# First transform of batch 0 with x as the stationary operand, its result kept on chip

## The chip, the cores and the metric

One core of a Trainium2 chip runs the whole program. The metric is the time on the device of one execution, in microseconds (us), lower is better. TensorE is called PE (its weight loads PEld), VectorE DVE, ScalarE ACT, GpSimd POOL and SyncE SP; SBUF is the memory on the chip, PSUM the accumulators that TensorE writes, DRAM the memory off the core.

## The reference

A two-dimensional Fourier transform of x, of which the real part is kept, is followed by two layers of two matrix products each.

```python
batch, seq, dim = (2, 3008, 256)
X = np.fft.fft(x, axis=1)
X = np.fft.fft(X, axis=2)
x = X.real.reshape(6016, 256)
h = x @ w_in                                     # 256 -> 2048
x = (np.maximum(h, 0.0) + alpha * np.minimum(h, 0.0)) @ w_out
h = x @ w_in2
out = (h * (1.0 / (1.0 + np.exp(-h)))) @ w_out2  # 2048 -> 256
```

## The kernel before, in words

The sequence transform of length 3008 = 47 * 64 is done as a transform of length 47 (stage A), one of length 64 (stage B), and the transform along the 256 columns is folded into the first weight matrix (`mix_w`: every pair of row blocks of `w_in` is multiplied with `cwt`). By symmetry 24 of the 47 rows and half of the columns are computed, in NC = 6 blocks c of 8 rows each: blocks 0 to 2 are batch 0, blocks 3 to 5 batch 1. A block has 512 columns of tokens, block 0 only 450.

Products of the layers are made in float32r in three passes: each operand is split in a high part (a copy by ACT into float32r) and a low part (the subtraction of the two on DVE or POOL). A float32 matmul that isn't split stands in the profile as two passes, each with a weight load of its own.

Before the loop over the blocks there is a front that prepares batch 0:

- Ten matmuls on zeros (`spin`) run while the first transfers land. Eight x tiles of 96 partitions x 1024 (`x`, 384 KB each) are loaded on SP's queue.
- Stage A, for each tile: ACT copies the high part (`xh`, L942), DVE subtracts the low part (`xl`, L943), PE makes 3 matmuls for each half tile with the constant `cat` as the stationary operand (`psA`, L355 to L357), ACT and DVE copy the result into `ev` (L960, L962).
- The result has the wrong axis on the partitions, so it goes through DRAM: `save_a` writes `tmid[0]`, `load_ur` reads it back turned as `ur` (in the place of `pq` of block 5). The table `QUEUE` says behind which tile each of these transfers is issued. The parts for blocks 1 and 2 are saved later (`save_a` with part 1 behind the loads of the front, `put` for part 2 in the loop) and loaded by `stage_b` with `load_u`.
- The first column pair of `w_in`, p = 0, is loaded as 64-bit words (`raw`), narrowed to float32 (`narrow`: ACT L211, L212, then DVE L217, L219, L221), and mixed (`psW` L512, `psS` L518). Fourteen and eight further `spin` matmuls stand around it.
- Stage B of block 0: 16 float32 matmuls `psB` (L984) with `ur` stationary, their split into `pq` (ACT L991, DVE L993), a row built on POOL (L979) and summed over the partitions by PE (`psP`, L995), copied into `pb`.

The loop `step1(c, m)` then runs 16 steps m for each block: 6 matmuls `psh` (L556), on DVE and ACT the activation (L564 to L570), `gh` and `gl` split on ACT and POOL (L586, L587), and 12 matmuls `pso` (L602) into `po`. Beside the steps of block 0 run what the later steps need, as jobs that `at(step, ...)` plans and that go on at named phases of a step: narrowing and mixing p = 2 to 7 of `w_in`, narrowing `w_out` in eight parts n (`narrow_wout`; part 0 at step 0; its split is ACT L265, POOL L266), stage B of block 1 (`stage_b` at steps 3, 6, 7, 9, then `rank_one`, which makes `pb` of block 1 through a small tensor `rd` in DRAM). Every engine works in the order in which the program is written. After the six blocks the second layer follows, in the same way.

Of the kernel before, what the change touches and what calls it, by code (L numbers as in the profile page):

```python
# [69 lines left out]
def _constants():  # L70
# [24 lines left out]
def kernel(  # L95
# [8 lines left out]
    ca: bass.AP,  # L104
    cb: bass.AP,
# [13 lines left out]
    psh = ctx.enter_context(tc.tile_pool(name="psh", bufs=1, space=PSUM, reuse_waits="tile"))  # L119
    pso = ctx.enter_context(tc.tile_pool(name="pso", bufs=4, space=PSUM, reuse_waits="tile"))  # L120

    tmid = [dram.tile([N2, 2 * CK * 2, P], F32, name=f"tmid{c}") for c in range(NC)]
# [9 lines left out]

    def place_pq(c):
        if c not in pq:
            pq[c] = keep.tile([P, 4, CK * N2], F32R, name=f"pq{c}", tag=f"px{c}")
        return pq[c]
# [196 lines left out]
    cbt = pf.tile([P, 2, N2], F32, name="cbt")  # L333
# [58 lines left out]
    def products_b(u):  # L392

        ps = ptile([P, KG, 2, N2], "psB")
        for k in range(KG):
            for eo in range(2):
                T.matmul(ps[:, k, eo], u[:, eo, k, :], cbt[:, eo], start=True, stop=True)  # L397
        return ps
# [21 lines left out]
    def stage_b(c, kk):  # L420
        while c >= NC // 2 and len(saved) < N2 // 4:
            yield EARLY
# [10 lines left out]
        pairs = list(parts_b(c, kk, products_b(u)))  # L433
# [15 lines left out]
    def rank_one(c):  # L449
# [4 lines left out]
        T.matmul(ps, u0, cbt[:, 0], start=True, stop=True)  # L454
# [44 lines left out]
    def mix_w(p, pool=None, tag="x"):  # L499
# [23 lines left out]
        if p < 2:  # L523

            column(pso.tile([P, 2, 2], F32, name="psS", tag="o"))
# [301 lines left out]
    def start_win2():  # L827
# [21 lines left out]
    SPIN = 10, 14, 8  # L849

    QUEUE = ((("s", 0, 8),), (("s", 8, 16),), (("s", 16, 24), ("w",), ("b",)), (("s", 24, 32), ("p", 0)),
             (("l", 0, 16, 0), ("s", 32, 40)), (("l", 16, 32, 0), ("s", 40, 48)), (("s", 48, 56), ("l", 32, 48, 0)),
# [288 lines left out]
```

## Time and profile before

| | |
|---|---|
| time, median of 3 runs | 984.4 us (982.74 to 984.95) |
| profiled execution: span from first to last instruction | 984.3 us |
| profiled execution: time of its own | not listed apart from the span |
| PE busy | 954.4 us, 97% of the span |
| PEld, DVE | 791.0 and 719.7 us |
| ACT, POOL | 598.0 and 508.6 us |
| moved by DMA | 52.72 MB |

The page names, for each engine, its busy time; the windows cut the span into stretches and give busy time and the granted TensorE clock of each; the chain follows the work that ended last back from the end; the timeline lists instructions in order of their start, with the idle time before them and what released them in brackets.

### The profile page before, as it was taken

To read this page: it belongs to the slowest core of one execution; us is meant where nothing else is said; L and a number is where in the kernel's file an instruction comes from. 1 tells how busy PE (TensorE), PEld (TensorE's weight loads), DVE (VectorE), ACT (ScalarE), POOL (GpSimd) and SP (SyncE) were. 2 spreads that over 40 slices of the span, in tenths; PEclk is the share of its full clock that TensorE was granted. 3 is DMA by queue.
4 is the path that set the end of the run, shared out by engine and by line. 5 is a ranking of instruction groups with operands and counts; after the bars stand their busy time and mean duration, and the time that the engine had idled before them with its cause. 6 is when DMAs were issued, how large, how long until landed. Compare 5 with 4: busy or idle time off the path is not lost.

```text
span 984.3 us, 12429 instructions
## 1 busy us (share of the span) xinstructions
PE 954.4 (97%) x4316; PEld 791.0 (80%) x4316; DVE 719.7 (73%) x1103; ACT 598.0 (61%) x1006; POOL 508.6 (52%) x328
## 2 busy tenths in 40 slices
PE   8799999999999999999999999999999999999998
PEld 5688878878878878778789988888888888888886
DVE  6698876778989989998766766576576566657554
ACT  6566566666656656665676565665566565556654
POOL 0154567765445556988996553354354354335322
PEclk9899999999999999999999999999999999999999
DMA  8921133323333220010011020010001001001001
GB/s 227 309 96 49 31 90 79 88 71 95 107 118 112 81 65 22 22 65 22 11 44 33 0 81 1 1 43 1 1 0 43 1 1 43 1 1 43 1 1 44
DMA packets 39407, 52.72 MB, mean 54 GB/s; under 512 B 3792, under 2 KB 22064, under 8 KB 39088
## 3 DMA queue, kind: packets, MB, share of 16 engines
q1 hardware_dynamic: 39056, 51.60, 17.1%
q8 instruction: 34, 0.56, 0.2%
q10 hardware_dynamic: 288, 0.33, 0.1%
q14 instruction: 29, 0.24, 0.1%
HBM read 35.26 MB, written 16.66 MB: 53 GB/s over the span
## 4 chain that ended last, share of the span: by engine, by line
PE 75%; DVE 9%; DMA 5%; ACT 4%; POOL 3%; issue 2%; SPq 1%; ACTq 0%; POOLq 0%; DVEq 0%
PE pso L790 26%; PE psh L722 23%; PE pso L602 15%; PE psh L556 8%; DVE r L570 4%; POOL gl L587 2%; ACT r L566 2%; DMA tmid<-ev 1%; DVE psh L565 1%; DMA stash_i<-y 1%; DMA stash_o<-y 1%; PE psB L397 1%; DMA raw<-in_w_in 1%; DVE h L564 1%; DVE y L221 1%
## 5 line engine op out<-in xcount | busy, mean ns | idle before, releaser
L743 DVE TENSOR_TENSOR ring<-ring,psh 128x512 f32<-128x512 f32 (+1 forms) x336 | 222.2, 674 | 167.5 <-PE psh L722 158.3
L790 PE MATMUL pso<-ghl,wAo 128*128 128x512 f32 (+1 forms) x1152 | 309.8, 385 | 0.0
L587 POOL TENSOR_TENSOR gl<-r,gh 128x1024 fp32r<-128x1024 f32 (+1 forms) x96 | 227.0, 2365 | 152.5 <-ACT gh L586 97.5
L722 PE MATMUL psh<-ts,wi 128*128 128x512 f32 (+1 forms) x1008 | 279.0, 385 | 0.0
L734 POOL TENSOR_TENSOR ghl<-ring,ghl 128x512 fp32r<-128x512 f32 (+1 forms) x96 | 137.1, 1429 | 252.6 <-ACT ghl L729 172.7
L790 PEld LDWEIGHTS pso<-ghl,wAo 128*128 128x128 f32 x1152 | 216.2, 188 | 40.7
L746 ACT ACTIVATE ring<-ring 128x512 f32<-128x512 f32 (+1 forms) x192 | 119.4, 622 | 176.4 <-DVE ring L743 174.6
L722 PEld LDWEIGHTS psh<-ts,wi 128*128 128x128 f32 x1008 | 189.1, 188 | 35.5 <-DVE r L570 0.3
L602 PE MATMUL pso<-gh,wo_o 128*128 128x512 f32 (+1 forms) x768 | 188.8, 386 | 3.0 <-POOL wo_o L266 2.9
L556 PE MATMUL psh<-pq,wa 128*128 128x512 f32 (+1 forms) x576 | 167.6, 400 | 4.7 <-DVE r L570 4.4
L602 PEld LDWEIGHTS pso<-gh,wo_o 128*128 128x128 f32 x768 | 144.2, 188 | 31.8 <-POOL wo_o L266 4.5
L570 DVE SCALAR_TENSOR_TENSOR r<-r,al,psh 128x512 f32<-128x512 f32 (+1 forms) x192 | 134.0, 734 | 17.8 <-ACT r L566 6.9
L586 ACT ACTIVATE gh<-r 128x1024 fp32r<-128x1024 f32 (+1 forms) x96 | 100.3, 1045 | 69.5 <-DVE r L570 69.1
L556 PEld LDWEIGHTS psh<-pq,wa 128*128 128x128 f32 x576 | 105.5, 190 | 29.7 <-DVE r L570 10.8
L729 ACT ACTIVATE ghl<-ring 128x512 fp32r<-128x512 f32 (+1 forms) x192 | 118.9, 619 | 6.2
L602 PE MATMUL pso<-gl,wo_o 128*128 128x512 f32 (+1 forms) x384 | 103.0, 390 | 2.9 <-POOL gl L587 2.9
L566 ACT ACTIVATE r<-psh 128x512 f32<-128x512 f32 (+1 forms) x96 | 56.5, 588 | 80.2 <-DVE psh L565 70.3
L565 DVE TENSOR_TENSOR psh<-h,psh 128x512 f32<-128x512 f32 (+1 forms) x96 | 65.8, 685 | 42.8 <-PE psh L556 37.4
L602 PEld LDWEIGHTS pso<-gl,wo_o 128*128 128x128 f32 x384 | 72.4, 189 | 18.5 <-POOL gl L587 4.6
L734 DVE TENSOR_TENSOR ghl<-ring,ghl 128x512 fp32r<-128x512 f32 (+1 forms) x96 | 77.2, 804 | 4.0 <-ACT ghl L729 3.5
L564 DVE SCALAR_TENSOR_TENSOR h<-pb,wst,psh 128x512 f32<-128x512 f32 (+1 forms) x96 | 69.9, 729 | 3.1 <-DMA pb<-rd 3.1
L567 DVE TENSOR_TENSOR psh<-h,psh 128x512 f32<-128x512 f32 (+1 forms) x96 | 65.2, 679 | 0.0
(94 smaller groups left out, 681.0 us busy)
## 6 DMA issues: line engine op xcount, KB each, us to landing
raw<-in_w_in SPq DMA_DIRECT2D x16, 512.0 KB, 6.2
raw<-in_w_out SPq DMA_DIRECT2D x16, 512.0 KB, 3.9
ur<-tmid SPq DMA_DIRECT2D x20, 256.0 KB, 3.3
out_dram<-ob SPq DMA_DIRECT2D x20, 256.0 KB, 2.2
tmid<-ev SPq DMA_DIRECT2D x50, 64.0 KB, 1.8
x<-in_x SPq DMA_DIRECT2D x8, 384.0 KB, 8.0
xr<-in_x SPq DMA_DIRECT2D x16, 192.0 KB, 2.4
tmid<-ev SPq DMA_DIRECT2D x23, 128.0 KB, 5.7
```

Of the source, the lines that this page charges most:

```text
L556: T.matmul(t[:, :w], wa[q][:, mm, eo, a, :], pq[c][:, 2 * eo + bb, :w], start=n == 0, stop=n == 2)
L564: V.scalar_tensor_tensor(t[:, :w], pb[c][:, :w], wst[:, m, 0:1], ps[0][:, :w], op0=ALU.mult, op1=ALU.add)
L570: V.scalar_tensor_tensor(r[:, s, :w], r[:, s, :w], al[:, m:m + 1], ps[s][:, :w], op0=ALU.mult, op1=ALU.add)
L586: A.activation(hi[:, :, :w], r[:, :, :w], AF.Copy)
L587: G.tensor_tensor(lo[:, :, :w], r[:, :, :w], f32(hi[:, :, :w]), op=ALU.subtract)
L602: T.matmul(po[c][s][k][:, :w], wo1[q][:, mm, a, k * P:(k + 1) * P], g[:, s, :w], start=m == 0 and a == 0 and g is hi, stop=m == NF - 1 and ...
L722: T.matmul(bank[j][:, :w], wi2[p][:, FORMS[j], a], t[:, :w], start=a == 0 and t is hi, stop=t is lo)
L729: A.activation(outs[p, i][:, 0, :w], g[:, :w], AF.Copy)
L734: eng.tensor_tensor(hl[:, 1, :w], g[:, :w], f32(hl[:, 0, :w]), op=ALU.subtract)
L743: V.tensor_tensor(dst[:, :w], a[:, :w], bank[j][:, :w], op=ALU.add)
L746: A.activation(a[:, :w], a[:, :w], AF.Silu)
L790: T.matmul(po[c, 2][s][k][:, :w], wo2[q][:, mm + m, a, k * P:(k + 1) * P], outs[p, i][:, g, :w], start=p == 0 and i < 2 and a == 0 and g == 0,
```

## The change

Stage A of batch 0 is turned round. The x tile is the stationary operand, in float32 and unsplit, and the constant (`a0`, 96 x 96) is the moving one, so that the result has the axis on the partitions that stage B wants. There are 64 such matmuls of 96 columns (`stage_u`, `psU`), in five units of 12 and one of 4; after each unit four copies (two on DVE, two on ACT, 64 partitions x 48 x n) put them into `u_all`, which holds blocks 0 to 2 on chip until step 26 of the loop (`set_apart` then gives its place to `pq` of blocks 3 to 5). The writes to and reads from `tmid` of blocks 0 to 2 go, and with them `ev`, the splits `xh` and `xl`, `QUEUE`, `put`, and the second and third group of `spin`. `tmid` stays for batch 1.

`cbt` gets a second form for the row order that results (`cbts`, 128 KB). The constants `cwt` and `cbts` are loaded on ACT's queue at the very start instead of behind the third tile. On SP's queue p = 0 of `w_in` stands behind the sixth x tile (`BEHIND`), and behind the eighth all other raw weights follow without waiting for anything. Part 0 of `w_out` is narrowed and split in the front (`wo0`), ahead of stage B's split, no longer at step 0. `take_in` moves from step 14 to step 27. `stage_b` of blocks 1 and 2 loads nothing, so it is one phase shorter.

```diff
+    a0 = a.reshape(2 * NP1, H1 // CK, 2, 2, CK).transpose(0, 2, 1, 3, 4).reshape(2 * NP1, -1).astype(np.float32)
...
+    three = tc.tile_pool(name="three", bufs=1, side="right", reuse_waits="tile")
+    u_all = three.__enter__().tile([P, 3, 2, CK, P], F32, name="u_all")
...
-        while c >= NC // 2 and len(saved) < N2 // 4:
+        while c >= HOST and len(saved) < N2 // 4:
...
-        u = pf.tile([P, 2, KG, P], F32, name="ur", tag="ur", bufs=2)
-        load_u(c, kk, u)
-        yield EARLY
+        if c < HOST:
+            u = u_all[:, c, :, kk:kk + KG]
+        else:
+            u = pf.tile([P, 2, KG, P], F32, name="ur", tag="ur", bufs=2)
+            load_u(c, kk, u)
+            yield EARLY
...
-    SPIN = 10, 14, 8
-
-    QUEUE = ((("s", 0, 8),), (("s", 8, 16),), (("s", 16, 24), ("w",), ("b",)), (("s", 24, 32), ("p", 0)),
...
+    SPIN = 10,
+
+    BEHIND = 5
+    UNITS = 12, 12, 12, 12, 12, 4
...
+        ac = wtile([2 * NP1, 2 * NP1], F32, "const", "y")
+        nc.sync.dma_start(ac, a0)
...
+            nc.sync.dma_start(xr[i], x[0, i])
+            if i == BEHIND:
+                next(first[0])
+        A.dma_start(cwt.rearrange("p k e j -> p (k e j)"), cw)
+        A.dma_start(cbts.rearrange("p a e k -> p (a e k)"), cb)
+        load_raw("o", 0)
+        next(first[1])
...
+        for kind, n in RAW_ORDER:
+            load_raw(kind, n)
...
+        def stage_u(n):
...
+            t = pp.tile([P, 3, 512], F32, name="psU", tag="u", bufs=2)
+            for j in range(n):
+                i, r = divmod(done + j, NX)
+                T.matmul(t[:, j // 4, j % 4 * 96:j % 4 * 96 + 96], xr[i][:, r], ac, start=True, stop=True)
+            v = t[:, :n // 4, :384].rearrange("p b (j m c) -> p b j m c", j=4, m=2)
+            for i, (half, m) in enumerate(((0, 0), (1, 0), (0, 1), (1, 1))):
+                src = v[half * N2:(half + 1) * N2, :, :, m].rearrange("p b j c -> p c b j")
+                dst = uv[m * N2:(m + 1) * N2, :, half, done:done + n].rearrange("p c (b j) -> p c b j", j=4)
+                if i % 2:
+                    A.activation(dst, src, AF.Copy)
                 else:
+                    V.tensor_copy(dst, src)
+            done += n
+
+        for i, n in enumerate(UNITS):
+            stage_u(n)
+            if i == 3:
+                run(first[0])
+            if i == 4:
+                run(mix_w(0, pp, "o"))
...
+        wo0 = narrow_wout(w_out, wo1, "wo1_", 0, 0, raws["o", 0])
...
+        run(wo0)
+        ur, cbt = u_all[:, 0], side(0)
...
-        for n in range(8):
+        for n in range(1, 8):
             at(WOUT[n], narrow_wout, w_out, wo1, "wo1_", n, 0, raws.get(("o", n)))
-        for i, n in enumerate(SAVES):
-            at(n, put, i)
-        at(14, take_in)
+        at(26, set_apart)
+        at(27, take_in)
```

On PE, the end of the front before, from the last x tile to the first step (names: `psA` stage A, `idle` the spins, `psW` and `psS` the mixing of p = 0, `psB` and `psP` stage B of block 0, `psh` the first step):

```order
L355 MATMUL psA<-xh_231,cat 96x512
L356 MATMUL psA<-xh_231,cat 96x512
L357 MATMUL psA<-xl_232,cat 96x512
L879 MATMUL idle<-zero 128x512 x14
L512 MATMUL psW<-wq,cwt 128x256 x4
L518 MATMUL psS<-ones,wq 128x2 x2
L879 MATMUL idle<-zero 128x512 x8
L984 MATMUL psB<-cbt,pq_112 128x64 x16
L995 MATMUL psP<-row_330,ones 128x512
L556 MATMUL psh<-pq_111,wa_310 128x450 x6
```

and the whole front of PE now:

```order
L894 MATMUL idle<-zero 128x512 x10
L937 MATMUL psU<-const,x_112 128x96 x16
L937 MATMUL psU<-const,x_115 128x96 x16
L937 MATMUL psU<-const,x_118 128x96 x16
L937 MATMUL psU<-const,x_123 128x96 x12
L531 MATMUL psW<-wq,cwt 128x256 x4
L537 MATMUL psS<-ones,wq 128x2 x2
L937 MATMUL psU<-const,x_123 128x96 x4
L968 MATMUL psB<-cbt,u_all 128x64 x16
L979 MATMUL psP<-row_277,ones 128x512
L575 MATMUL psh<-pq_111,wa_239 128x450 x6
```

The 48 matmuls `psA` and 22 of the spins are gone, 64 `psU` have come, and the mixing of p = 0 stands ahead of the last four of them.

On ACT, from the mixing of p = 0 to the splits of stage B, before (`wa` and `wst` are the mixed weights, `pq` the split of stage B):

```order
L960 ACTIVATE ev_235<-psA 96x512
L514 ACTIVATE wa_310<-psW 128x2x2x128
L519 ACTIVATE wst<-psS 128x4
L991 ACTIVATE pq_111<-psB 128x192
L991 ACTIVATE pq_111<-psB 128x256
```

and now, where `y` and `raw` are part 0 of `w_out` while it is narrowed, and `wo_o` its high half:

```order
L533 ACTIVATE wa_239<-psW 128x2x2x128
L538 ACTIVATE wst<-psS 128x4
L943 ACTIVATE u_all<-psU 64x48x4 x2
L224 ACTIVATE y_267<-raw_128 128x512
L225 ACTIVATE raw_128<-raw_128 128x512
L278 ACTIVATE wo_o_273<-y_267 128x2x256
L975 ACTIVATE pq_111<-psB 128x192
L975 ACTIVATE pq_111<-psB 128x256
```

Part 0 of `w_out` and the last copies of `u_all` have moved ahead of the first split of stage B.

On DVE, step 0 of the loop before, from the two halves of the activation (`r`) to the low part of the mixed weights (`wa`); `wq` is p = 2 of `w_in`, `y_376` part 0 of `w_out`:

```order
L570 SCALAR_TENSOR_TENSOR r<-r,al,psh 128x450
L217 TENSOR_SCALAR wq<-wq 128x512
L217 TENSOR_SCALAR y_376<-y_376 128x512
L570 SCALAR_TENSOR_TENSOR r<-r,al,psh 128x450
L219 ISA wq<-raw_272,wq 128x1024
L219 ISA y_376<-raw_270,y_376 128x1024
L221 SCALAR_TENSOR_TENSOR wq<-raw_272,wq 128x512
L221 SCALAR_TENSOR_TENSOR y_376<-raw_270,y_376 128x512
L527 TENSOR_TENSOR wa_310<-psW,wa_310 128x2x2x128
```

and now:

```order
L589 SCALAR_TENSOR_TENSOR r<-r,al,psh 128x450
L230 TENSOR_SCALAR wq<-wq 128x512
L589 SCALAR_TENSOR_TENSOR r<-r,al,psh 128x450
L232 ISA wq<-raw_135,wq 128x1024
L234 SCALAR_TENSOR_TENSOR wq<-raw_135,wq 128x512
L546 TENSOR_TENSOR wa_239<-psW,wa_239 128x2x2x128
```

The three instructions of part 0 of `w_out` no longer stand between those of p = 2.

## Rows read from the trace of the kernel before

**Rows 1.** The page's first part: busy us of each engine, share, instructions.

```profile
PE 954.4 (97%) x4316; PEld 791.0 (80%) x4316; DVE 719.7 (73%) x1103; ACT 598.0 (61%) x1006; POOL 508.6 (52%) x328
```

**Rows 2.** Windows: stretch, length, busy us by engine (instructions), clock, DMA share, GB/s.

```profile
45.00:50.00 5.00, 5.00 (x15) 4.17 (x15) 4.78 (x9) 4.28 (x8) 1.35 (x2) 0.58 1.05 379
...
131.00:200.00 69.00, 68.53 (x317) 55.56 (x316) 49.65 (x77) 45.96 (x76) 47.62 (x26) 1.00 0.29 76
```

**Rows 3.** Chain that ended last, first 60 us: start, us, what.

```profile
11.41 6.02 DMA tmid<-ev
...
27.54 8.00 DMA raw<-in_w_in
```

**Rows 4.** DMA in the first 60 us, 40 slices of 1.5 us: GB/s.

```profile
GB/s 0 238 251 265 246 232 238 240 240 225 356 347 312 222 102 194 33 210 207 323 329 283 306 346 326 212 305 360 359 399 401 388 348 399 351 400 90 0 0 0
```

**Rows 5.** Timeline of the front: start, us, engine, line, operation [idle before].

```profile
1.45 4.12 PE L879 MATMUL idle<-zero 128*128 128x512 f32 x10 [1.45 <-DVE zero L872]
...
24.11 1.89 PE L512 MATMUL psW<-wq,cwt 128*128 128x256 f32 x8
...
25.84 0.50 PE L518 MATMUL psS<-ones,wq 128*128 128x2 f32 x4
...
28.14 3.68 PE L984 MATMUL psB<-cbt,pq 128*128 128x64 f32 x32
...
29.47 1.06 POOL L979 TENSOR_TENSOR row<-pq,cbt 128x512 f32<-128x512 f32 x1 [29.03 <-DMA pq<-tmid]
...
31.66 1.08 PE L995 MATMUL psP<-row,ones 128*128 128x512 f32 x2
31.86 0.70 ACT L991 ACTIVATE pq<-psB 128x192 fp32r<-128x192 f32 x3 [1.09 <-PE psB L984]
...
32.17 1.78 PE L556 MATMUL psh<-pq,wa 128*128 128x450 f32 x6
...
32.59 0.79 DVE L993 TENSOR_TENSOR pq<-psB,pq 128x192 fp32r<-128x192 f32 x3 [1.00 <-ACT pq L991]
...
33.37 0.67 ACT L211 ACTIVATE wq<-raw 128x512 f32<-128x512 f32 x1
...
35.36 0.69 DVE L221 SCALAR_TENSOR_TENSOR wq<-raw,wq 128x512 int32<-128x512 int32 x1
```

**Rows 6.** Lines by form in the first 60 us: busy us, mean ns, idle before.

```profile
L962 DVE COPY ev<-psA 96x512 f32<-96x512 f32 x8 | 5.4, 680 | 0.7 <-PE psA L357 0.7
L960 ACT ACTIVATE ev<-psA 96x512 f32<-96x512 f32 x8 | 4.7, 590 | 1.1 <-PE psA L357 1.0
```

**Rows 7.** Timeline of steps 0 and 1.

```profile
39.40 0.42 DVE L217 TENSOR_SCALAR y<-y 128x512 int32<-128x512 int32 x1
...
40.93 0.68 DVE L219 CUSTOM_DVE_ANT_0 y<-raw,y 128x1024 uint16<-128x1024 uint16 x1
...
41.48 2.08 POOL L587 TENSOR_TENSOR gl<-r,gh 128x900 fp32r<-128x900 f32 x1 [10.95 <-ACT gh L586]
41.53 2.57 DVE L221 SCALAR_TENSOR_TENSOR wq<-raw,wq 128x512 int32<-128x512 int32 x1
...
44.03 0.68 DVE L221 SCALAR_TENSOR_TENSOR y<-raw,y 128x512 int32<-128x512 int32 x1
44.16 3.78 PE L512 MATMUL psW<-wq,cwt 128*128 128x256 f32 x8 [4.08 <-DVE wq L221]
...
44.74 0.63 ACT L265 ACTIVATE wo_o<-y 128x512 fp32r<-128x512 f32 x1 [3.34 <-DVE y L221]
...
45.45 1.28 POOL L266 TENSOR_TENSOR wo_o<-y,wo_o 128x512 fp32r<-128x512 f32 x1 [1.89 <-ACT wo_o L265]
...
48.89 0.96 ACT L586 ACTIVATE gh<-r 128x900 fp32r<-128x900 f32 x1 [0.32 <-DVE r L570]
```

**Rows 8.** Timeline where block 1 begins.

```profile
127.36 1.69 PE L602 MATMUL pso<-gh,wo_o 128*128 128x450 f32 x7 [1.36 <-POOL wo_o L266]
...
130.00 0.75 DVE L564 SCALAR_TENSOR_TENSOR h<-pb,wst,psh 128x512 f32<-128x512 f32 x1 [3.09 <-DMA pb<-rd]
```

More of the change, by code (lines that the diff above doesn't have):

```diff
@@ L117 @@
     dram = ctx.enter_context(tc.tile_pool(name="dram", bufs=1, space=DRAM))
-    psh = ctx.enter_context(tc.tile_pool(name="psh", bufs=1, space=PSUM, reuse_waits="tile"))
-    pso = ctx.enter_context(tc.tile_pool(name="pso", bufs=4, space=PSUM, reuse_waits="tile"))
-    tmid = [dram.tile([N2, 2 * CK * 2, P], F32, name=f"tmid{c}") for c in range(NC)]
+    tmid = {c: dram.tile([N2, 2 * CK * 2, P], F32, name=f"tmid{c}") for c in range(HOST, NC)}
     aside = dram.tile([P, 2, 2, CK * N2], F32, name="aside")
@@ L332 @@
     cat = pf.tile([2 * NP1, 2, 96], F32R, name="cat")
-    cbt = pf.tile([P, 2, N2], F32, name="cbt")
+    cbts = pf.tile([P, 2, 2, N2], F32, name="cbt")
     cwt = pf.tile([P, 2, 2, P], F32, name="cwt")
@@ L390, in load_u, with side, products_b @@
         nc.sync.dma_start(t, src.rearrange("p (e k) j -> p e k j", e=2)[:, :, kk:kk + KG])
-    def products_b(u):
+    def side(c):
+        return cbts[:, 1 if c < HOST else 0]
+    def products_b(c, u):
         ps = ptile([P, KG, 2, N2], "psB")
@@ L396, in products_b @@
             for eo in range(2):
-                T.matmul(ps[:, k, eo], u[:, eo, k, :], cbt[:, eo], start=True, stop=True)
+                T.matmul(ps[:, k, eo], u[:, eo, k, :], side(c)[:, eo], start=True, stop=True)
         return ps
@@ L453, in rank_one @@
         ps = ptile([P, N2], "psR")
-        T.matmul(ps, u0, cbt[:, 0], start=True, stop=True)
+        T.matmul(ps, u0, side(c)[:, 0], start=True, stop=True)
         ranked.add(c)
@@ L523, in mix_w @@
         if p < 2:
-            column(pso.tile([P, 2, 2], F32, name="psS", tag="o"))
+            column(pool.tile([P, 2, 2], F32, name="psS", tag=tag))
         yield BANK
@@ L874 @@
         V.memset(u0, 0.0)
-        idle = pso.tile([P, 512], F32, name="idle", tag="o")
+        pre = tc.tile_pool(name="pre", bufs=2, space=PSUM, reuse_waits="tile")
+        pp = pre.__enter__()
+        idle = pp.tile([P, 512], F32, name="idle", tag="o")
         def spin(n):
@@ L967 @@
-        ur = ur.rearrange("p (e k) j -> p e k j", e=2)
-        for kind, n in (("i", 2), ("o", 1)):
-            load_raw(kind, n)
-        for i in range(nx):
-            save_a(0, i * NX, NX, evs[i], (1,))
-        for kind, n in LATER:
-            load_raw(kind, n)
-        run(first[0])
-        spin(SPIN[1])
-        run(mix_w(0, pso, "o"))
-        spin(SPIN[2])
+                t = keep.tile([2 * NP1, 2, NX, P], F32, name="x0", tag=f"wo1_{i // 2}")
+            xr.append(t[:, i % 2])
@@ new lines @@
+        for i, n in enumerate(UNITS):
[4 more added lines that the diff above has]
+                run(mix_w(0, pp, "o"))
+        assert done == N2
+        wo0 = narrow_wout(w_out, wo1, "wo1_", 0, 0, raws["o", 0])
+        pre.__exit__(None, None, None)
+        psh = ctx.enter_context(tc.tile_pool(name="psh", bufs=1, space=PSUM, reuse_waits="tile"))
+        pso = ctx.enter_context(tc.tile_pool(name="pso", bufs=4, space=PSUM, reuse_waits="tile"))
@@ L1046 @@
                 close1(last)
-                if c * NF + m in WARM:
-                    idle = pso.tile([P, 512], F32, name="idle", tag="o")
-                    for _ in range(WARM[c * NF + m]):
-                        T.matmul(idle[:, :_width(c)], wa[0][:, 0, 0, 0, :], pq[c][:, 0, :_width(c)], start=True, stop=True)
                 last = step1(c, m)
```

112 lines of the change are left out of this document (32 added, 80 removed).

## The prediction

> **What bounds the kernel now.** I read the engine shares first: PE is busy 954.4 us of a span of 984.3 [rows 1], so no more than 29.9 us of idle time can be won anywhere without taking matmuls away. Then the windows, to see where that idle time lies. From 131 us on there is hardly any: PE is busy 68.53 of 69 us at the full clock [rows 2]. What is gained before 131 us is therefore kept to the end, and what is changed behind it is paid in matmul time alone; the order of PE's work there stays as it was. So the question is how much earlier block 1 begins, and for that I read the chain and the timeline of the first 50 us. The reader should see that the front waits for transfers, not for arithmetic: single pieces of the chain are 6.02 us for a write of `tmid` and 8.00 us for a raw weight that queues behind it [rows 3]. And step 0 of the loop has a hole: PE waits 4.08 us for the narrowed p = 2, at 44.16 us, and comes back at half the clock, 8 passes of the mixing in 3.78 us where 1.89 were enough at 24.11 [rows 5, 7]; the window shows a granted clock of 0.58, a mixture of the levels 1.2 and 2.4 GHz [rows 2].
>
> **The new stage A.** Nothing in the trace is a float32 matmul of 96 columns, so I bound it. Each float32 matmul is two passes. Passes of 64 columns start every 3.68/32 = 0.115 us, passes of 2 columns every 0.50/4 = 0.125, passes of 256 columns every 1.89/8 = 0.236 [rows 5]. Since 2 columns are no cheaper than 64, the weight load sets the pace there; 96 columns cost 0.115 if it still does, and 0.135 on a straight line from 64 to 256 (0.115 + 32/192 x 0.121). I take 0.115: the 64-column row is the nearest, and 96 columns by the slope of the widest passes (0.236/256 each) stream in 0.09. So 64 matmuls, 128 passes, cost 14.7 us, at most 17.3. Below that they cannot go by much, since x must land: before, x alone came at about 243 GB/s [rows 4]; now `a0` (0.04 MB), `cwt` and `cbts` (0.39 MB), x (3.15 MB) and p = 0 (0.52 MB) share the queues, 4.10 MB or 16.9 us. From about 2 us, where bytes begin to flow, that is 18.9 us for the eighth tile and 13.5 us for the sixth.
>
> At this place the Trainium skill speaks against the change: its page "TensorE: Matmul & The Clock Gate" (section "HAM oscillation — how this bites in real kernels") says that matmul bursts which each wait for their next operand's transfer begin at half the clock every time. Here each 8 matmuls are fed by one x tile; 8 x 0.23 = 1.8 us of work against 0.39 MB / 243 = 1.6 us of transfer, so by the rows the burst is not shorter than the wait and the stage stays dense. By the rule's case the stage would run at twice the time, which is the slow rival below.
>
> **The front, step by step.** The ten spins end at 1.45 + 4.12 = 5.6 us [rows 5]; `a0`, the first tile and a like share of the constants (0.8 MB) have landed at about 5.4. The first 48 matmuls run until 5.6 + 11.0 = 16.6. Each unit of 12 takes PE 2.8 us and leaves two copies of 576 elements to DVE and two to ACT; from 680 and 590 ns for 512 [rows 6] that is some 0.75 and 0.65 each, 1.5 us a unit, hidden beside PE. A source with a stride of 96 is not in the trace; if it doubled the copies (3.0 us a unit) they would bind and cost 5 x 0.2 + 1.5 = 2.5 us; I take the rows as they are, because the copies of `psA` are from PSUM too. Behind the fourth unit, at 18.1, ACT starts narrowing p = 0, which takes 2.7 us end to end (33.37 to 36.05 for p = 1 [rows 5]): 20.8. It has landed at 15.6. PE meanwhile finishes the fifth unit at 19.8 (0.4 us late for the eighth tile) and waits one us. Mixing (24.11 to 26.34, 2.2 us) ends at 23.0, the last four matmuls at 23.9, their copies at 24.7.
>
> Then stage B of block 0 takes 3.7 us of PE, to 28.4. ACT and DVE meanwhile narrow part 0 of `w_out`: 2.7 us, then 0.63 for the high half [rows 7], to 28.0. The splits into `pq` queue behind it on ACT (0.70 each half, then 0.79 on DVE [rows 5]) and end at 30.3. POOL takes 1.28 for the low half [rows 7], to 29.3, and only then builds the row (1.06), to 30.4; before, nothing stood ahead of the row. The first step's matmuls follow 0.51 us behind the start of `psP` (31.66 to 32.17): 30.9 against 32.17 [rows 5]. **Term 1: 1.3 us.** The 22 spins (they filled gaps) and the DRAM way are gone, but the narrowing of part 0 has come in.
>
> **Step 0.** Part 0 of `w_out` was also narrowed here. DVE's three instructions 0.42, 0.68 and 0.68 [rows 7] go, less about 0.08 of overlap each: 1.5 us. And L221 of p = 2 took 2.57 us here instead of 0.69 [rows 5, 7], beside POOL's L587 that had started 0.05 us earlier: the two held each other up for 1.9 us. Without L219 of part 0 in between, this L221 starts 0.6 us behind the second half of the activation, while the `gh` that POOL waits for takes 0.96 [rows 7]. So L221 goes ahead of POOL and runs in 0.69. **Term 2: 1.5 + 1.9 = 3.4 us** at the start of step 1's activation, and from there to `gh` of step 1 (48.89 [rows 7]) nothing else is late: `psh` of step 1 is long done, the raw weights are on chip by about 35 us at the rates of [rows 4], and POOL is free. PE's hole shrinks from 4.08 us to about 1, so the half clock behind it should go too; I count that at nothing, because DVE, not PE, is late there.
>
> **The rest.** In the steps up to 126 us the order on DVE, ACT and POOL is the same ring (activation, `gh`, `gl`), so the 4.7 us pass through. Stage B of block 1 loses its loads, runs at steps closer together, and `pb` is asked for earlier, in front of three saves of batch 1. Before, DVE waited 3.09 us for `pb` at 130.00; but PE had its last wait of 1.36 us at 127.36 for a split on POOL, and worked on through DVE's wait [rows 8]. So I count that at nothing, with 0 to 1.4 as its bounds. `take_in` at step 27 lies beside a full PE: nothing.
>
> Sum: 984.3 - 1.3 - 3.4 = 979.6 by the span; the median of the runs is 0.1 above it, so **979.7 us**.
>
> **The rivals.** (a) The front is not shortened. The queue now carries 0.9 MB more before the last x tile; copies of double length cost 2.5 us, passes of 0.135 up to 2.6 us. With either, term 1 turns to -1.2, and with part of term 2 lost (POOL gets in ahead of L221 again, 1.9) the time is 982 to 984. For it: every step of my front rests on an estimate. Against: term 2 doesn't depend on it.
>
> (b) More is won: `pb` in time (up to 1.4), and x and the constants landing at the 350 GB/s of the later slices [rows 4] instead of 243, which takes up to 2 us off the front: 976 to 978. Against: the x transfers alone never went over 265 [rows 4].
>
> (c) The clock. Stage A's passes load weights most of the time; if the clock falls there, as it did after 4.08 us of idleness at 44 us, each pass doubles (1.89 to 3.78 [rows 5, 7]). With all 128 passes, 14.7 us more; if it holds until the mixing and then falls, because the spins that covered these waits are gone, mixing, the last four matmuls and stage B cost 2.2 + 0.9 + 3.7 = 6.8 more. That is 986 to 994, slower than before. It decides from 4.7/0.115 = 41 passes at half clock. For it: waits of 1 us before the mixing and 2 us before `psP` have no spin in them now. Against: the wait is half of the one that let the clock fall, and the 32 dense passes of `psB` [rows 5] were no slower at their end.
>
> **Chances.** Forecast 0.53 (978 to 981.5), (a) 0.20, (b) 0.13, (c) 0.14. What a measurement can tell from no change is 0.2%, 2 us, so faster is below 982.4. (a) divides evenly between faster and the same: faster 0.53 + 0.13 + 0.10 = 0.76; same 0.10 and a little of (c), 0.12; slower 0.12. The range must reach into (a) fully and some way into (b) and (c): 975.5 to 986.5.
>
> **What would show it.** Right: 128 passes of L937 about 0.115 us apart at clock 1.00; the first `psh` near 31 us; L234 of p = 2 at 0.69; `gh` of step 1 near 44; block 1's first activation 4 to 5 us earlier; equal PE time behind it. Wrong: a granted clock under 0.9 between 6 and 30 us; copies to `u_all` over 1 us; a row on POOL after 32; or a front that is shorter while block 1 begins when it did, because the ring of steps 1 to 15 takes the gain back.

## The result: 992.8 us, slower by 0.85%

The changed kernel took 992.82 us in the median of 4 runs (992.17 to 993.09), the kernel before 984.67 beside it (982.74 to 985.13): the ratio is 1.0085, with a 95% interval of 1.007 to 1.010. The forecast of 979.7 us missed by 13 us and on the wrong side. The profiled execution of the changed kernel took 992.17 us, its span is 990.4 us, 6.1 more than before.

First the engine shares of the page after the change, against [rows 1]:

```profile
PE 960.8 (97%) x4374; PEld 798.8 (81%) x4374; DVE 711.6 (72%) x1099; ACT 592.9 (60%) x1002; POOL 509.6 (51%) x328
```

PE is busy 6.4 us longer, about as much as the span has grown, while DVE and ACT have less to do. So in sum it is not new waiting that made it slower: PE's matmuls take longer, although 48 `psA` and 22 spins have gone and only 64 `psU` have come. The windows show where (columns as in [rows 2]):

```profile
20.00:25.00 5.00, 2.53 (x11) 2.00 (x11) 3.04 (x5) 2.23 (x4) 0.00 (x0) 0.76 1.05 373
25.00:30.00 5.00, 3.46 (x20) 3.05 (x19) 1.56 (x4) 2.60 (x7) 0.00 (x0) 0.84 1.05 387
30.00:35.00 5.00, 5.00 (x26) 5.00 (x25) 2.77 (x7) 1.91 (x6) 2.22 (x2) 0.50 0.78 286
35.00:40.00 5.00, 5.00 (x15) 3.61 (x14) 1.19 (x4) 2.40 (x8) 0.07 (x1) 0.53 0.00 0
70.00:75.00 5.00, 5.00 (x18) 4.21 (x17) 4.07 (x7) 2.78 (x7) 1.76 (x2) 0.66 0.00 0
600.00:700.00 100.00, 100.00 (x440) 82.11 (x439) 62.13 (x93) 57.27 (x96) 41.12 (x29) 1.00 0.03 11
```

Two places stand out. From 30 to 40 us the granted clock is at its lower level, 1.2 GHz, nearly all the time (0.50 and 0.53), and for a part of the windows from 20, 25 and 70 us too. And from 600 to 700 us, in the second layer that the change does not touch, PE is full at the full clock and still makes only 440 matmuls in 100 us; the same window of the kernel before has this row:

```profile
600.00:700.00 100.00, 100.00 (x443) 82.80 (x442) 63.36 (x95) 58.41 (x98) 39.29 (x29) 1.00 0.03 11
```

The front in the timeline after the change, against [rows 5]:

```profile
5.74 5.79 PE L937 MATMUL psU<-const,x 96*128 96x96 f32 x48
...
8.88 0.75 DVE L945 COPY u_all<-psU 64x576 f32<-64x576 f32 x1 [7.34 <-PE psU L937]
9.67 0.65 ACT L943 ACTIVATE u_all<-psU 64x576 f32<-64x576 f32 x1 [6.72 <-DVE u_all L945]
10.35 0.75 DVE L945 COPY u_all<-psU 64x576 f32<-64x576 f32 x1 [0.71 <-ACT u_all L943]
11.13 0.65 ACT L943 ACTIVATE u_all<-psU 64x576 f32<-64x576 f32 x1 [0.82 <-DVE u_all L945]
...
22.37 0.69 DVE L234 SCALAR_TENSOR_TENSOR wq<-raw,wq 128x512 int32<-128x512 int32 x1
...
23.11 3.42 PE L531 MATMUL psW<-wq,cwt 128*128 128x256 f32 x8 [2.47 <-DVE wq L234]
...
26.73 1.11 PE L937 MATMUL psU<-const,x 96*128 96x96 f32 x8
29.39 7.06 PE L968 MATMUL psB<-cbt,u_all 128*128 128x64 f32 x32 [1.54 <-ACT u_all L943]
...
36.24 2.02 PE L979 MATMUL psP<-row,ones 128*128 128x512 f32 x2
37.27 2.92 PE L575 MATMUL psh<-pq,wa 128*128 128x450 f32 x6
```

The reader is to see the brackets of the four copies: each was released by the copy of the other engine. DVE and ACT take turns, and a unit costs 8.88 to 11.78, 2.9 us, where two engines side by side would need 1.5. The narrowing of p = 0 queues behind them, PE waits 2.47 us for it, and behind that wait most of the mixing (3.42 us instead of 1.89 [rows 5]) and, after a short stretch at full speed, psB run at half the clock (7.06 us for the 32 passes that took 3.68 [rows 5]). The first psh stands at 37.27, 5.1 us later than the 32.17 of before.

Step 0, against [rows 7]:

```profile
45.25 0.95 ACT L605 ACTIVATE gh<-r 128x900 fp32r<-128x900 f32 x1 [0.60 <-DVE r L589]
45.85 0.69 DVE L234 SCALAR_TENSOR_TENSOR wq<-raw,wq 128x512 int32<-128x512 int32 x1
46.28 2.23 POOL L606 TENSOR_TENSOR gl<-r,gh 128x900 fp32r<-128x900 f32 x1 [11.22 <-ACT gh L605]
46.60 1.78 PE L531 MATMUL psW<-wq,cwt 128*128 128x256 f32 x7 [1.30 <-DVE wq L234]
```

Here it went as forecast: L234 takes 0.69 ahead of POOL instead of 2.57 beside it, and PE waits 1.30 us instead of 4.08. The `gh` of step 1 follows at 50.74.

To see where time comes and goes, the start of the high split on ACT (`gh`, in the second layer `ghl`) of the same step is compared between traces. In the table, worked out from those starts, a number is the start in that kernel less the start in the kernel before, in us (the kernels in the other columns are the experiments below):

```
step (start before)     after  e1_aligned  e6_banks  e9_row  e11_early  e7_weights
0    (40.4)              +4.8     +4.8       +3.8     -2.3     -2.4       +0.2
1    (48.9)              +1.9     +1.8       +0.9     -5.3     -5.3       +0.2
5    (71.7)              +3.3     +1.8       +2.3     -3.9     -3.9       +0.4
22   (164.5)             +2.4     +2.7       +1.7     -2.9     -4.2       +0.7
46   (278.2)             +1.1     +1.6       +0.8     -3.3     -5.9       +0.2
94   (490.0)             +3.7     +2.3       +1.4     -3.0     -5.1       +2.2
last of layer 2 (973.8)  +6.1     +2.4       +1.2     -3.2     -4.7      +11.8
```

A trace is one execution, and half-clock stretches fall in other places from one execution to the next: e2_shift below, which runs the instructions of the kernel before and is as fast by its median, stands at -0.3 at step 1 and at -2.8 from step 46 on, and the trace of e6_banks is that of an execution 2.7 us above its median. So a difference of up to 3 us between two columns need not belong to the kernels; the medians decide.

The changed kernel is 4.8 us late at step 0, wins 3.0 back by step 1 (4.81 to 1.85, term 2 of the prediction), loses 1.5 by step 5 (the half clock in the window from 70 us), is 1.1 us late at step 46, and then falls behind by another 5 us over 700 us in which no instruction was changed. So two causes had to be found: one in the front, one in the long stretch behind it.

### The profile page after: what moved, and what is told of

It is laid out like the page before. It is cut to its first block, busy times and chain, and to the rows that moved or that the text cites. A ratio compares the mean times of both kernels' runs of the same rounds, so it can differ in the third digit from the quotient of the medians.

```text
span 990.4 us, 12453 instructions
## 1 busy us (share of the span) xinstructions
PE 960.8 (97%) x4374; PEld 798.8 (81%) x4374; DVE 711.6 (72%) x1099; ACT 592.9 (60%) x1002; POOL 509.6 (51%) x328
## 4 chain that ended last, share of the span: by engine, by line
PE 80%; DVE 8%; ACT 4%; POOL 3%; issue 2%; DMA 1%; SPq 0%; ACTq 0%; DVEq 0%; POOLq 0%
PE pso L809 26%; PE psh L741 23%; PE pso L621 18%; PE psh L575 9%; DVE r L589 3%; POOL gl L606 2%; ACT r L585 2%; DVE psh L584 1%; PE psB L413 1%; PE psW L531 1%; ACT gh L605 1%; PE psB L968 1%; PE psU L937 1%; DVE h L583 1%; DVE x L633 1%
```

## The experiments

**Is it where the tiles lie?** With `u_all` on the right side of SBUF, the tiles that take its place later (`pq` of blocks 3 to 5, two slots of `ts` in the second layer) begin 32 bytes past a multiple of 64, while all weights begin on one. Before the change every operand of these matmuls began on a multiple of 64. So 576 matmuls have their two operands at different places within 64 bytes: 288 `psh` of blocks 3 to 5 and 288 of the second layer. e1_aligned puts 32 unused bytes ahead on the right side; e2_shift does the same to the kernel before, so that the operands of the two layers, weights and moving ones alike, all begin 32 past one.

```diff
+    edge = ctx.enter_context(tc.tile_pool(name="edge", bufs=1, side="right", reuse_waits="tile"))
+    edge.tile([P, 8], F32, name="edge")
     three = tc.tile_pool(name="three", bufs=1, side="right", reuse_waits="tile")
```

> The changed kernel with an unused tile of 32 bytes ahead of u_all on the right side of SBUF, so that u_all and what takes its place later (pq of blocks 3 to 5, two kinds of tiles of the second layer) begin at a multiple of 64 bytes instead of 32 past one. Nothing else differs. In the changed kernel's trace a psh matmul of block 5, whose moving operand lies there, starts every 236 ns and one of the kernel before every 227, and the second kernel falls behind by 2.8 us in the second layer's blocks 1 to 5. Theory A (the place costs, 480 matmuls of 512 columns with 32 past 64): psh of block 5 back at 227 ns, the second layer as long as before, time 992.8 - 4 to 5 = about 988. Rival B (the clock or the chip was a little slower in that run): no change, 992.8 within 1.

```diff
+    keep.tile([P, 8], F32, name="edge")
     al = keep.tile([P, NF], F32, name="al")
```

> The kernel before with an unused tile of 32 bytes ahead of all tiles in SBUF, so that nearly all operands of all matmuls, moving and stationary, begin 32 bytes past a multiple of 64. Theory A: 3321 moving operands of 512 columns and 648 narrower ones cost 9 to 15 ns each, 35 to 55 us in all, less what idle time hides: 1015 to 1035. Rival B: 984.7 within 2.

e1_aligned took 989.36 us (ratio 1.0045, 1.0027 to 1.0062), 3.5 us under the changed kernel. Its column in the table stays where it is from step 94 to the end (+2.3, +2.4). But e2_shift took 985.86 (1.0007, 0.9998 to 1.0016): nothing, where 30 us and more were expected. The theory that a place off the multiple of 64 costs by itself fell. What was left is that the place counts only against that of the other operand, so a third kernel shifted the weights alone: `wa` of the first layer and the weights of the second product of the second layer.

```diff
+                if tag == "wA":
+                    dst[q] = keep.tile([P, 2064], F32R, name=f"{tag}o{q}", tag=f"{tag}{q}")[:, 8:2056].rearrange("p (a b d) -> p a b d", a=4, b=2)
...
-            wa[q] = keep.tile([P, 4, 2, 2, P], F32R, name=f"wa{q}", tag=f"wA{q}")
+            wa[q] = keep.tile([P, 2064], F32R, name=f"wa{q}", tag=f"wA{q}")[:, 8:2056].rearrange("p (a b c d) -> p a b c d", a=4, b=2, c=2)
...
```

> The kernel before with the tiles of wa (first layer) and of w_out of the second layer begun 32 bytes past a multiple of 64; all moving operands stay on multiples of 64. Theory 'relative' (a matmul pays when its stationary and its moving operand differ in their place within 64 bytes): 576 + 1,152 = 1,728 matmuls pay; in the changed kernel 576 such matmuls cost 3.7 us, 6.5 ns each, so here 11 us, about 996, psh of the first layer and pso of the second at up to 236 ns from start to start, and psh of the second layer beside them at a little over 227. Rival 'alternation' (it is the change from a moving operand at one place to one at another that costs): nothing, 985. Rival 'moving' (only the moving operand's own place counts, and all tiles shifted together were free for another reason): nothing, 985.

998.85 us (1.0142, 1.0126 to 1.0159): 13.1 more than the 985.79 of the kernel before beside it, a little over the 11 expected for 576 + 1,152 such matmuls. Both rivals said nothing would happen. The same window in e1_aligned, e2_shift and e7_weights, in this order:

```profile
600.00:700.00 100.00, 100.00 (x443) 82.81 (x442) 62.63 (x93) 57.40 (x97) 40.80 (x29) 1.00 0.03 11
```

```profile
600.00:700.00 100.00, 100.00 (x443) 82.81 (x442) 62.89 (x95) 57.98 (x97) 40.06 (x28) 1.00 0.03 11
```

```profile
600.00:700.00 100.00, 100.00 (x433) 80.94 (x432) 61.24 (x91) 56.78 (x96) 40.54 (x29) 1.00 0.03 11
```

443 matmuls where the two operands stand alike, on a multiple of 64 or 32 past one; 433 where one of the two products of the layer has them unlike; 440 in the changed kernel, where a part of the first product has. By forms, `psh` of block 5 (455 to 494 us) takes 389 ns in the kernel before and 396 in the changed one; `pso` beside it, none of whose operands moved, goes from 389 to 392 (before and after, in that order):

```profile
L602 PE MATMUL pso<-gh,wo_o 128*128 128x512 f32 x74 | 18.4, 389 | 0.0
L556 PE MATMUL psh<-pq,wa 128*128 128x512 f32 x54 | 15.2, 389 | 0.0
```

```profile
L621 PE MATMUL pso<-gh,wo_o 128*128 128x512 f32 x78 | 19.5, 392 | 0.0
L575 PE MATMUL psh<-pq,wa 128*128 128x512 f32 x54 | 15.5, 396 | 0.0
```

So the price is not paid by the matmuls with unlike operands alone; a part of it falls on their neighbours.

**Do the copies wait because both write one tile?** e3_two_tiles splits `u_all` into two tiles of 24 rows, one for each engine.

```diff
-    u_all = three.__enter__().tile([P, 3, 2, CK, P], F32, name="u_all")
+    pool3 = three.__enter__()
+    u_two = [pool3.tile([P, 3 * CK, P], F32, name=f"u_all{g}") for g in range(2)]
...
+            for half, m in ((0, 0), (1, 0), (0, 1), (1, 1)):
+                for g in range(2):
...
+                    if g:
+                        A.activation(dst, src, AF.Copy)
+                    else:
+                        V.tensor_copy(dst, src)
```

> The changed kernel with u_all as two tiles of 24 rows each, one written by DVE alone and one by ACT alone; a unit is eight copies of half the size, four on either engine. In the changed kernel's trace the four copies of a unit wait for one another in turn (DVE 0.75, ACT 0.65, DVE, ACT: 2.9 us a unit), though they write different places, and what stands behind them, the narrowing of p = 0, is late; PE then idles for 2.5 us and runs at half the clock for most of the next 15. Theory C (the tile's order makes them wait): the copies of a unit side by side in 1.8 us, p = 0 narrowed by 21 instead of 23, PE not at half the clock at stage B (psB in 3.7 us, not 7.1), first psh at 31 instead of 37.3, and 3 to 6 us less: 987 to 990. Rival D (the clock falls anyway, from the waits before psP and the first steps): copies side by side, but psB still in 7 us, gain under 2.5.

1001.8 us (1.0154, 1.0136 to 1.0172), 9 us worse than the changed kernel. Its timeline says why:

```profile
9.24 0.45 DVE L953 COPY u_all<-psU 64x288 f32<-64x288 f32 x1 [7.69 <-PE psU L944]
9.72 0.40 ACT L951 ACTIVATE u_all<-psU 64x288 f32<-64x288 f32 x1 [6.77 <-DVE u_all L953]
10.16 0.46 DVE L953 COPY u_all<-psU 64x288 f32<-64x288 f32 x1 [0.47 <-ACT u_all L951]
...
12.96 15.14 PE L944 MATMUL psU<-const,x 96*128 96x96 f32 x72 [1.08 <-ACT u_all L951]
```

Each engine writes a tile of its own and they still take turns. So the tile they write is not the reason; what they share is `psU`, the PSUM tile of three banks that they read. Eight short copies in a row take longer than four, PE waits 1.08 us for a free `psU`, and the 72 passes behind that wait take 15.14 us, 0.21 each, at half the clock, where the 48 of the changed kernel had taken 5.79, 0.12 each.

**Are the removed spins missing?** e4_spins puts nine spins ahead of the mixing and six ahead of stage B.

```diff
             if i == 4:
+                spin(9)
                 run(mix_w(0, pp, "o"))
         assert done == N2
+        idle = pp.tile([P, 512], F32, name="idle", tag="o")
+        spin(6)
```

> The changed kernel with nine matmuls on zeros ahead of the mixing of p = 0 and six ahead of stage B of block 0, where PE waits; the copies stay as they are. It tells what the clock alone costs. Theory C: the waits stay (p = 0 narrowed at 23), but the mixing takes 1.9 us instead of 3.4 and psB 3.7 instead of 7.1, so the first psh comes 3 to 5 us earlier, and the time is 2 to 4 us less: 989 to 991. If the half clock costs nothing, because DVE and ACT are late anyway: 992.8 within 1.

991.67 us (1.0063, 1.0050 to 1.0076), 1.2 under the changed kernel, less than the 2 to 4 expected, and with intervals that overlap hardly clear of the noise:

```profile
23.07 1.99 PE L531 MATMUL psW<-wq,cwt 128*128 128x256 f32 x8 [0.35 <-DVE wq L234]
...
28.57 3.79 PE L971 MATMUL psB<-cbt,u_all 128*128 128x64 f32 x32 [0.36 <-ACT u_all L943]
...
34.30 2.08 PE L982 MATMUL psP<-row,ones 128*128 128x512 f32 x2 [1.94 <-POOL row L966]
...
39.78 3.78 PE L531 MATMUL psW<-wq,cwt 128*128 128x256 f32 x8 [1.15 <-DVE wq L234]
```

Mixing and psB run at full speed, but psB starts no earlier than 28.57 (29.39 without the spins), because it waits for the copies. Behind it PE now waits 1.94 us for POOL's row, which stands behind the low half of part 0, and the half clock comes there. The spins move the slow stretch; they don't remove it.

**Copies from banks of their own.** e6_banks is e1_aligned with sixteen units of four matmuls, each in one PSUM bank; one engine makes all four copies of a unit, and units alternate.

```diff
+            t = pp.tile([P, 512], F32, name="psU", tag="u", bufs=6)
+            for j in range(4):
...
+            for half, m in ((0, 0), (1, 0), (0, 1), (1, 1)):
...
+                if g % 2:
+                    A.activation(dst, src, AF.Copy)
+                else:
+                    V.tensor_copy(dst, src)
...
+            if i == 11:
                 run(first[0])
...
+            if i == 14:
                 run(mix_w(0, pp, "o"))
```

> The aligned kernel with stage A in sixteen units of four matmuls, each with a PSUM bank of its own, all four copies of a unit on one engine, units alternating between DVE and ACT; p = 0 narrowed behind the twelfth unit, mixing issued behind the fifteenth. Theory 'bank' (the two engines' copies stood in line because both read the same PSUM bank): no copy waits for the other engine; each unit's copies take 4 x 0.34 = 1.36 us, so 0.68 us a unit over two engines, less than PE's 0.93; the 128 passes run without a stop from 5.7 to 20.6, L234 of p = 0 ends by 20, the last copies by 24.5, psB runs at 3.7 us, the first psh stands near 31.5 instead of 37.3, gh of step 0 about 1 us before that of the kernel before, gh of step 1 about 4 us before it. If steps 1 to 17 keep it, the time is 5 to 6 us under the aligned kernel's: 984. If, as in the aligned kernel and the one with spins, 1.5 to 2.5 us are lost again at the start of block 1 (PE waits for the split on POOL), 985 to 986. Rival 'tile' (the order comes from the one tile u_all): the copies still wait for each other, now 64 copies of 0.34 one after another, 21.8 us, and the front gets longer: over 993.

984.61 us (0.9999, 0.9986 to 1.0013): level with the kernel before, 4.8 us under e1_aligned.

```profile
5.84 13.62 PE L938 MATMUL psU<-const,x 96*128 96x96 f32 x120 [0.38 <-DMA x<-in_x]
6.98 1.46 DVE L946 COPY u_all<-psU 64x192 f32<-64x192 f32 x4 [5.43 <-PE psU L938]
7.87 1.33 ACT L944 ACTIVATE u_all<-psU 64x192 f32<-64x192 f32 x4 [4.92 <-PE psU L938]
...
20.91 3.08 PE L533 MATMUL psW<-wq,cwt 128*128 128x256 f32 x8 [1.45 <-DVE wq L236]
...
27.91 7.09 PE L969 MATMUL psB<-cbt,u_all 128*128 128x64 f32 x32 [1.42 <-ACT u_all L944]
```

The copies overlap and are released by PE alone, and 120 passes run in one piece, 0.1135 us each. The one tile `u_all` is still written by both engines. That settles that the shared `psU` put the copies in order; whether tile or bank decides is not shown, because in this kernel each unit has a tile and a bank of its own. The profile also shows that the front was not yet mended: behind a wait of 1.45 us the mixing took 3.08 and psB 7.09, so the first psh came at 35.83, not 31.5. The expectation had the median right, but for the profiled execution, which took 987.33 us, it missed the clock.

The Trainium skill, page "PSUM — Partial Sum Buffer", section "PSUM bank collisions raise a hardware error", has a rule that comes near this: two engines must not touch one bank in the same 32 partitions at once, reads against reads included, so programs put an order between them; in different banks they may run together. The trace agrees in so far as there are turns of 0.7 to 0.8 us where the banks are shared and none where they aren't. But by the page different partitions of one bank may be read together, and here DVE reads partitions 0 to 63 and ACT 64 to 127: the order in this kernel is coarser than the rule asks, and no run here shows whether the finer one would hold.

**Row and spins.** e9_row adds to e6_banks POOL's row ahead of part 0 and four spins ahead of psB (the short copy into `cat` moves behind part 0 with it); e10_spins also nine spins ahead of the mixing.

```diff
+        idle = pp.tile([P, 512], F32, name="idle", tag="o")
+        spin(4)
...
-        run(wo0)
...
         G.tensor_tensor(row, ur[:, 1, :, 0:1].to_broadcast([P, CK, N2]),
                         cbt[:, 0:1].to_broadcast([P, CK, N2]), op=ALU.mult)
+        run(wo0)
```

> As the kernel with a bank for each unit, with POOL's row issued ahead of the narrowing of part 0 and four spins ahead of psB. Theory 'bank': the row no longer stands behind the low half of part 0, psP follows psB at once, first psh at 30 to 30.5, gh of step 1 about 5 us before that of the kernel before; 1 us less than the kernel with banks alone, 983 if the steps behind keep it, 985 if block 1's start takes it back. Rival: the splits into pq, not the row, are last: same as the kernel with banks alone.

982.38 us (0.9982, 0.9959 to 1.0006), 2.2 under e6_banks:

```profile
8.02 1.06 POOL L964 TENSOR_TENSOR row<-u_all,cbt 128x512 f32<-128x512 f32 x1 [7.58 <-DVE u_all L946]
...
21.31 2.00 PE L533 MATMUL psW<-wq,cwt 128*128 128x256 f32 x8 [0.65 <-DVE wq L236]
...
26.04 3.79 PE L971 MATMUL psB<-cbt,u_all 128*128 128x64 f32 x32 [0.47 <-ACT u_all L944]
...
30.18 1.97 PE L577 MATMUL psh<-pq,wa 128*128 128x450 f32 x6
```

The row needs only the first column of `u_all` and is done at 9 us. The first psh stands at 30.18, and `gh` of step 1 is 5.3 us earlier than before. By step 22 only 2.9 of that are left.

```diff
             if i == 14:
+                spin(9)
                 run(mix_w(0, pp, "o"))
```

> As the kernel with a bank for each unit, the early row and four spins, with nine more spins ahead of the mixing of p = 0. Theory: what varies from run to run there is the clock; a wait of 0.65 us ahead of the mixing left it at full speed in one kernel, 1.45 us in another was followed by 3.08 instead of 2.00 us for the mixing and by 7.09 for psB. With spins in that wait the mixing takes 2.0 us and psB 3.8 in the profile, and the median falls by 0 to 1 us: 981.5 to 982.4. Rival: the spins are still running when the narrowed weights arrive and put the mixing off: 983.

982.66 us (0.9976, 0.9960 to 0.9993). Against e9_row nothing can be told: the spins cost nothing and win nothing there.

**Is term 2 real?** e8_back is e1_aligned with part 0 of `w_out` narrowed at step 0 again.

```diff
-        wo0 = narrow_wout(w_out, wo1, "wo1_", 0, 0, raws["o", 0])
...
-        run(wo0)
...
-        for n in range(1, 8):
+        for n in range(8):
```

> The aligned kernel with the narrowing of part 0 of w_out put back into step 0, where the kernel before has it. By term 2 of the prediction the 2.95 us that step 0 had won come back: gh of step 1 less gh of step 0 is 8.4 us again instead of 5.5, with L221 (here the narrowing's last instruction of p = 2) stretched beside POOL. Without the narrowing the front is shorter: POOL's row stands 1.3 us earlier, the splits start at the end of psB's first half, gh of step 0 comes 1.5 to 2.5 us earlier. Sum 0.5 to 1.5 us more than the aligned kernel: 990 to 991. Rival: the narrowing in the front costs as much as it saves in step 0 (3 us): the same time, 989.4. Rival: the hole in step 0 does not come back because PE now runs late: 987.

992.01 us (1.0068, 1.0055 to 1.0082), 2.7 more than e1_aligned. By the profiles its `gh` of step 0 is 1.1 us later than that of e1_aligned, and in step 0 the 3.0 us of term 2 are lost:

```profile
47.30 2.08 POOL L608 TENSOR_TENSOR gl<-r,gh 128x900 fp32r<-128x900 f32 x1 [34.41 <-ACT gh L607]
47.35 2.57 DVE L236 SCALAR_TENSOR_TENSOR wq<-raw,wq 128x512 int32<-128x512 int32 x1
...
49.98 2.50 PE L533 MATMUL psW<-wq,cwt 128*128 128x256 f32 x5 [3.99 <-DVE wq L236]
```

DVE's last instruction of p = 2 again takes 2.57 us beside POOL, and PE's hole is back at 3.99 us. The expectation was 1 to 2 us too low: it had the front shorter without part 0, but psB, at half the clock, was last there anyway.

**Where does the rest go, and does it belong to the change?** In e10_spins PE waits 1.43 and 1.77 us for the low halves of parts 6 and 7 of `w_out`, the second of them here:

```profile
123.56 2.01 PE L623 MATMUL pso<-gh,wo_o 128*128 128x450 f32 x7 [1.77 <-POOL wo_o L281]
```

e11_early narrows these two a step earlier; e13_before_early does that to the kernel before; e12_unaligned takes e10_spins without the 32 bytes.

```diff
-    WOUT = 0, 1, 3, 5, 5, 7, 9, 11
+    WOUT = 0, 1, 3, 5, 5, 7, 8, 10
```

> As e10_spins, with parts 6 and 7 of w_out narrowed a step earlier (WOUT 8 and 10 for 9 and 11). Theory: two to three of the microseconds won by step 1 are lost again at steps 14 to 17, because PE waits 1.4 and 1.8 us for the low halves of these parts on POOL and runs on at half the clock; without these waits they are kept: 2 us less than e10_spins, 980. Rival: another operand (gl, pb, the activation) is late at the same place, and the time is that of e10_spins.

> The kernel before with parts 6 and 7 of w_out narrowed a step earlier, and nothing else. It tells whether what e11_early wins belongs to the change. In the kernel before PE waits 1.18 and 1.36 us for these two halves, and DVE 3.09 for pb right behind. If pb is what holds block 1 there, nothing is won: 985. If the waits are, 1 to 2.5 us: 983.

> As e10_spins without the unused 32 bytes, so that pq3, pq4, pq5 and two slots of ts begin 32 bytes past a multiple of 64 again while their weights stand on one. If the price of the placement and that of the front add up, 3.5 us more than e10_spins: 985.5. Rival: the placement costs only where PE has no slack, and an earlier start of block 1 hides part of it: 1.5 to 2.5 more.

e11_early: 981.44 us (0.9971, 0.9956 to 0.9987), the fastest of all, 3.5 us under the kernel before. Of the 2 us expected against e10_spins 1.2 came, and the intervals overlap. In its profile the two waits are gone, but PE now waits 2.30 us at 99.54 for `pq` and 1.66 us at 117.59 for the activation, both on DVE. The start of block 1, 125 to 130 us, in e10_spins and then in e11_early:

```profile
125.00:130.00 5.00, 5.00 (x22) 4.33 (x21) 2.99 (x5) 1.87 (x5) 0.93 (x1) 0.68 0.00 0
```

```profile
125.00:130.00 5.00, 5.00 (x29) 4.55 (x28) 3.84 (x7) 3.52 (x6) 2.25 (x2) 1.00 0.00 0
```

e13_before_early: 991.25 us (1.0071, 1.0047 to 1.0096), 6 us slower where 0 to 2.5 faster were expected:

```profile
112.95 1.29 POOL L349 TENSOR_TENSOR xhl<-xr,xhl 96x512 fp32r<-96x512 f32 x1 [0.64 <-ACT xhl L345]
113.12 1.67 DVE L219 CUSTOM_DVE_ANT_0 y<-raw,y 128x1024 uint16<-128x1024 uint16 x1
...
114.32 2.41 POOL L587 TENSOR_TENSOR gl<-r,gh 128x900 fp32r<-128x900 f32 x1
114.83 2.45 DVE L221 SCALAR_TENSOR_TENSOR y<-raw,y 128x512 int32<-128x512 int32 x1
...
117.67 1.01 PE L518 MATMUL psS<-ones,wq 128*128 128x2 f32 x4 [3.48 <-DVE pq L416]
```

The earlier narrowing meets POOL's instructions and is stretched from 0.68 to 1.67 and 2.45 us; `pq` queues behind it, PE waits 3.48 us. It is the mechanism of term 2, set off in another place. So the kernel before gains nothing by the same edit.

e12_unaligned: 987.07 us (1.0032, 1.0015 to 1.0049), 4.4 more than e10_spins. The price of the placement is the same, or a little more, with the front mended: it adds up, and the rival by which an earlier block 1 hides a part of it is out.

## Why the prediction was wrong

**Stage A, the passes: right.** 48 passes in 5.79 us are 0.12 each at the full clock, 0.1135 in e6_banks; forecast 0.115. The case of the Trainium skill's rule that the prediction weighed against the change, bursts that each wait for a transfer, did not come about: between 5.74 and 20.65 us PE waited twice, 0.30 us each time, and for copies.

**The front, the copies: the step that failed.** "... two copies of 576 elements to DVE and two to ACT ... 1.5 us a unit, hidden beside PE." Each copy took what the prediction said, 0.75 and 0.65; but they are not beside each other: 2.9 us a unit. It had asked whether a copy gets longer (a stride of 96), not whether the two engines may read `psU` at the same time. Its rival (a) had the right price for a unit of 3.0 us, 2.5, for another reason: p = 0 was narrowed by 23.06 instead of 20.8, 2.3 us late. What that rival did not carry on is what stands behind: the wait of one us ahead of the mixing became 2.47, the clock fell there, and the last copies ended at 29.4 instead of 24.7. Term 1 came out as +5.1 instead of -1.3 us at the first psh.

**The clock, rival (c): it happened, a part of it.** Its sign, a granted clock under 0.9 ahead of 30 us, is there (0.76 and 0.84). Stage A held the clock and it fell at the mixing, as the rival has it; mixing and psB took 3.42 + 7.06 where 2.0 + 3.8 are full speed (e4_spins), 4.7 more. That the time fell in its range, 986 to 994, is in part luck: with spins only 1.2 us came back, and 3.5 us are a cost that no rival had. The forecast had counted the fall as unlikely, because a wait of one us was well under the 4.08 at 44 us; but in the profile of e6_banks 1.45 us were followed by the lower clock, and the first psh stood at 35.83 with the copies side by side. So copies as forecast would not have been enough for the forecast's 30.9; e9_row, with 0.65 us ahead of the mixing, the row out of the way and spins ahead of psB, has 30.18.

**Term 2: right.** 3.0 us won by step 1 against 3.4 forecast, and e8_back gives these 3.0 away when part 0 goes back. One reading in it was off: the two did not hold each other up, DVE alone was held. POOL took 2.08 us beside L221 [rows 7] and 2.23 without it.

**"What is changed behind it is paid in matmul time alone": wrong, by 4 us.** The prediction took matmul time as given by the shapes, and so all that follows the start of block 1 as equal. 576 matmuls got another placement of their operands. 992.82 - 989.36 = 3.5 us, and e12_unaligned less e10_spins = 4.4: 6 to 8 ns for each of them, neighbours included; e7_weights gives 13.1 us / 1,728 = 7.6 ns.

**Block 1.** `pb` is early, as forecast (no wait of DVE for it at 129.31), but PE waits there for POOL: 1.78 us instead of 1.36 [rows 8]. With the front mended, this wait and half a clock behind it take back about 2 of the 5 us in the traces of e9_row and e10_spins (by `gh`, 1.8 between steps 15 and 20). The prediction had counted this at nothing, and had named it only at its end as a thing to watch.

The sum by medians: 992.8 less 3.5 for the placement (e1_aligned), 4.8 for the turns of the copies and the clock that fell with them (e6_banks) and 2.2 for row and spins leads to the 982.4 of e9_row. The forecast, 979.7, is still 2.7 below that. In the trace of e9_row 1.4 us are lost by step 5 and 1.8 between steps 15 and 20; that this is the whole of the rest is not shown.

## What to carry to other kernels

Before two engines are counted side by side, ask what they read as well as what they write: here two engines that read one PSUM tile took turns, and a tile and a bank for each was a small edit. When a change moves tiles, compare the start addresses of both operands of the matmuls that it doesn't touch. And where a front gets dense, look which waits are left ahead of a long run of matmuls, since a wait costs more than its length if the clock falls behind it.

## What was not expected of the hardware

- A float32r matmul of 512 columns whose moving operand begins 32 bytes past a multiple of 64 while its stationary one begins on a multiple, or the other way round, costs 6 to 8 ns more by the medians, of 227 from start to start. In the second layer, where PE is full, it is more: from the first `ghl` to the last the changed kernel falls from +3.3 to +6.1, 2.8 us for 288 such matmuls, and e7_weights from +1.9 to +11.8, 9.9 us for 1,152, so 9.7 and 8.6 ns each. A part of it shows in the neighbours, whose operands are alike. With both operands at the same place, on a multiple or 32 past one, nothing is paid. Why is open: no run separates the weight load from the streaming.
- The clock does not follow the length of a wait alone. Behind 1.08 us (e3_two_tiles) and 1.45 us (e6_banks) of idle PE it fell to the lower level, behind 0.65 us (e9_row) it stayed at the full one; and in step 0 a wait of 1.99 us was followed by a mixing of 1.99 us in e10_spins, one of 1.98 by 2.85 in e9_row.
- DVE's combination of `raw` and `wq` takes 0.69 us by itself, and 2.45 to 2.57 when POOL's split has started just before. The Trainium skill, page "SBUF — State Buffer", section "SBUF: two separate sides", calls it a lock on ports that either DVE, with two inputs from SBUF, or POOL holds for a whole instruction, whichever started first. The rows agree: in e8_back POOL ends at 49.38, and DVE, begun 0.05 us behind it, half a microsecond later, at 49.92; in e13_before_early, where POOL had begun 0.51 us earlier, they end at 116.73 and 117.28.
